# Three chained blocks on one core: the first weights split over two queues, sums of weights by accumulating transfers, and three pieces of early work moved

## The chip, the cores and the metric

The kernel runs on one core of a Trainium2 chip. The metric is the device time of one execution, in microseconds (us). A core has five engines with instruction streams of their own: PE (TensorE, matrix products), DVE (VectorE), ACT (ScalarE), POOL (GpSimd) and SP (SyncE, which here only issues transfers). They meet through semaphores alone. Data live in SBUF; products land in PSUM, 8 banks of 128 x 512 words here.

## The reference

Three blocks follow each other. Attention, with 4 batches, 8 heads, 512 tokens, 32 states and width 64, reads in both directions:

```python
scores = scale * x @ state.T;  a = softmax(scores);   xread = a @ state
scores2 = scale * state @ x.T; a2 = softmax(scores2); sread = a2 @ x
x = concat([xread, sread]) laid out as 2176 rows of 512
```

Then two feed-forward blocks:

```python
x = ((x @ w_a) * (x @ w_b)) @ w_out         # 512 -> 1536 -> 512
h = x @ w_in                                # 512 -> 2048
out = (max(h, 0) + log1p(exp(-abs(h)))) @ w_out2
```

Weights and results have twice the words that fp32 needs: the loaded weights are read as pairs of 32-bit words, a low and a high one, and turned into fp32 on the chip.

## The kernel before, in words

All work is written down as steps of a planner (class `Plan`, lines 156 to 330) in the order of the program. A step has a cost per engine that may do it, the buffers that it reads and writes, and a rank, its place in the program. `go` then goes through modelled time: whenever an engine is free, it gets the ready step of the lowest rank for which buffers can be found. The result is a fixed order of instructions for each engine; at run time the engines follow these orders and wait on semaphores. A step that writes a buffer comes behind every earlier step that wrote the same buffer. Buffers are slots of 128 x 512 words: `SF` holds fp32 (36 slots), `SR` the rounded parts that PE multiplies (58 slots), `PS` is PSUM.

Weights come in 34 units (line 548 on): `ab` (s, 0 and 2), four of the eight quarters of `w_a` and `w_b` that part s of the 1536 columns needs, 6 parts; `wo` (s), the rows of `w_out` of that part; then `in` and `out` for the last block, 8 each. `load` (517) issues the transfers of a unit, on SP except for the very first unit, which both go out on ACT's queue. `fetch` (569) loads whatever stands ahead of a unit in the list and hands the unit to `convert` (529): one ACT activation and, on DVE, two tensor_scalars (line 443), two scalar_tensor_tensors (447) and a tensor_tensor (435, called at 543) that adds the value `v` and the low part `e`. `split` (509) then makes of the sum a rounded high part (a cast on ACT or DVE, 427) and a low rest (a tensor_tensor on DVE or POOL, 435). A product of two split operands is three matmuls (`three`, 484); where an operand is left whole it is one product in full fp32.

At the start x and state arrive (`load_x`, 586). `scores_of` (653) turns x and multiplies it with the state; `state_softmax` (731) makes the softmax over the states, 6 DVE operations of full size among others, and for batches 0 and 1 (`G32`) keeps the result whole for part 0, while `A_later` holds the step that splits it for the parts after. `sread` (682) does the other direction. `state_w` (770) and, from part 1 on, `state_rows` (799) multiply the state with the weights; the results of `state_rows` are laid out by 8 copies of 128 KB on SP for each call. The main loop (979 to 1022) goes over the 6 parts and the 4 batches; `gates_of` (870) computes a part's two products for a batch and multiplies them on DVE (line 887). `y_part` (898) adds the part's share of y. The last block follows (1028 to 1111).

What sets the order around the change: the program's order of the steps `bring_wo(0)`, `bring(s + 1, ...)` and `A_later[b]()`; the queue of SP, which is in order and holds loads and copies alike; and the planner's costs for a transfer (`go`, lines 288 to 290): it lands 1.8 us after its issue plus its bytes at 350 GB/s plus 0.7.

Of the kernel before, what the change touches and what calls it, by code (L numbers as in the profile page):

```python
# [16 lines left out]

P = 128
W = 512
NF_SLOTS = 36  # L20
NR_SLOTS = 58

# [95 lines left out]
def made(x):  # L120
    return x.ap() if isinstance(x, Ref) else x
# [212 lines left out]
def attention_moe_moe2(ctx, tc, x, state, w_a, w_b, w_out, w_in, w_out2, out):  # L334
# [98 lines left out]
    def tt(o, a, b, op):  # L433
        n, ps = cols(o), in_psum(a, b)
        put = lambda eng: lambda: eng.tensor_tensor(  # L435
            out=made(o), in0=made(a), in1=made(b), op=op)
        ways = {"dve": (dve_us(n, True), put(nc.vector), *([] if ps else [True]))}
        if not ps:
            ways["pool"] = (0.23 + 0.00215 * n, put(nc.gpsimd))
        plan.add(ways, [a, b], [o])  # L440
# [19 lines left out]
    def transfer(size, *pairs, act=False):  # L460

        def give():
            for o, i in pairs:
                (nc.scalar if act else nc.sync).dma_start(out=made(o), in_=made(i))  # L464

        ways = {"sp": (0.48 * len(pairs), give, size)}
        if act:
            ways = {"act": (0.45 * len(pairs), give, size, "dma")}
        plan.add(ways, [i for _, i in pairs], [o for o, _ in pairs])

    class Products:


# [40 lines left out]

    raws = []

    def load(n, *srcs, act=False):

        b = Buf(F, 2 * n, RAW_SPARE)
        words = b.all().rearrange("p a b -> p (a b)").bitcast(U32)  # L520
        pairs = []
        for i, src in enumerate(srcs):
            src = src.rearrange("(k p) c -> p k c", p=P).bitcast(U32)
            dst = words.rearrange("p (k i c) -> p k i c", i=len(srcs), k=src.shape[1])
            pairs.append((dst[:, :, i, :], src))
        transfer(2 * n * W * P * 4, *pairs, act=act)
        return b

    def convert(b, spare=0):

        run = b.run // 2
        words = b.all().rearrange("p a b -> p (a b)").bitcast(U32)
        words = words.rearrange("p (c t) -> p c t", t=2)
        low, high = words[:, :, 0], words[:, :, 1]
        v, e = Buf(F, run, spare + run), Buf(F, run, spare)
        v_, e_ = (i.all().rearrange("p a b -> p (a b)") for i in (v, e))
        vu, eu = v_.bitcast(U32), e_.bitcast(U32)
        activation(v_, high.bitcast(F32), AF.Copy, scale=2.0 ** -112)
        ts(vu, vu, 3, ALU.logical_shift_left)
        stt(vu, high, 0x80000000, vu, ALU.bitwise_and, ALU.bitwise_or)  # L540
        ts(eu, vu, 0xFF800000, ALU.bitwise_and)
        stt(e_, low, 2.0 ** -52, e_, ALU.mult, ALU.mult)
        tt(v_, v_, e_, ALU.add)
        return v


# [21 lines left out]

    def fetch(key, spare=0):
        load_to(key)  # L570
        return convert(loaded.pop(key), spare)


    key = order.pop(0)
    loaded[key] = load(*units[key], act=True)
    zs = Buf(F, 1)
    transfer(10 * NS * DM * 4, *(
        (zs[0][NS * b:NS * b + NS].rearrange("p (h d) -> p h d", h=H),
# [74 lines left out]
    def scores_of(b):  # L653

        xT = []
        for g in range(2):
            ps = turned(xs[b], 2 * g)
            xT.append(Buf(F, 2))  # L660
            copy(xT[g].all(), ps.all())
        banks = Buf(K, 2)
        for g in range(2):
            m = Products()
            for i in range(4):
                at = quarter(b, i)
                j, i2 = divmod(i, 2)
                for half in range(2):
                    rows = slice(64 * half, 64 * half + 64)
                    m.one(  # L670
                        banks[half][32 * at:32 * at + 32, g * HW:g * HW + HW],
                        srow(sts[i2 ^ half], 2 * g + j, half, NS * b, NS),
                        xT[g][j][rows, i2 * HW:i2 * HW + HW], True, True, us=0.06,
                        tile_position=(64 * half, 32 * at),
                    )
            m.end()
        raw[b] = Buf(F, 2)
        both = raw[b].all().rearrange("p g (c h n) -> p g c h n", h=2, n=P)
        for half in range(2):
            copy(both[:, :, :, half], banks[half].rearrange("p (g c n) -> p g c n", g=2, n=P))  # L680
# [85 lines left out]
    def bring(s, p):  # L766

        ab[s, p] = ab[s, p + 1] = fetch(("ab", s, p), 4)
# [101 lines left out]
    def gates_of(s, b):  # L870

        m_ = [sw.pop((s, b, g)) for g in range(2)]
        if s:
            m_ = [(i[0], i[1]) for i in m_]
        t = Buf(F, 2)
        for i in range(2):
            ps = Buf(K, 2)
            for k in range(2):
                m = Products()
                c = slice(i * HW + k * P, i * HW + k * P + P)  # L880
                for g in range(2):
                    m.three(ps[k], [q[:, c] for q in m_[g]], A[b][g], g == 0, g == 1)
                m.end()
            if i == 0:
                copy(t.all(), ps.all())
            else:
                tt(t.all(), t.all(), ps.all(), ALU.mult)
        if s == 0 and b in G32:
            A_later[b]()
        return (t,) if s == 0 and b in Y32 else split(t)  # L890

    def add_up(dst, ps, new):
# [86 lines left out]
    for s, b in steps:  # L979
        if s == 0 and b == 0:  # L980
            scores_of(1)
        hl = gates_of(s, b)
        if s == 0:
            if b == 0:
                bring_wo(0)
                state_softmax(1)
                scores_of(2)
                state_w(0, 1, 0)
                state_w(0, 1, 1)
            if b == 1:  # L990
                state_softmax(2)
                scores_of(3)
            if b == 2:
                state_softmax(3)
        if s == SREAD:
            sread(b)
        if s and b == 0:
            if s > SREAD + 1:
                read_x(s)
            bring_wo(s)  # L1000
        if s == SREAD + 1 and b < SREAD + 2:
            read_x(b)
        if s == SREAD + 1 and b == 3:
            for t in range(SREAD + 1):
                read_y(t)
        if s > SREAD and b == 2:
            read_y(s)
        if s + 1 < NHS:
            if b == 0:
                bring(s + 1, 0)  # L1010
            if b == 1:
                bring(s + 1, 2)
                state_rows(s + 1, 0)
            if b == 2:
                state_rows(s + 1, 1)
                state_rows(s + 1, 2)
            if b == 3:
                state_rows(s + 1, 3)
        elif b:
            bring_w2(("in", 0) if b == 1 else ("out", 0) if b == 2 else ("in", 1))  # L1020
        pend.append((s, b, hl))
        if len(pend) > 1:
            finish()
# [122 lines left out]
```

## Time and profile before

| | |
|---|---|
| median of 3 runs | 746.11 us (745.89 to 746.93) |
| profiled execution | 746.87 us, span of its instructions 745.1 us |
| busy: PE, DVE, ACT, POOL | 723.4, 594.3, 409.4, 9.0 us |
| bytes moved by DMA | 66.15 MB, mean 89 GB/s |
| chain that ended last | PE 90%, DVE 4%, SP's queue 2%, DMA 2% |

The span is the time from the first to the last instruction in the trace; the execution's own time has 1.8 us more around it. Busy times are of one execution. An engine that is busy all the time in a stretch sets the length of that stretch; one with idle time waits there for another, and the trace names whom.

### The profile page before, as it was taken

To read this page: it belongs to the slowest core of one execution; us is meant where nothing else is said; L and a number is where in the kernel's file an instruction comes from. 1 tells how busy PE (TensorE), PEld (TensorE's weight loads), DVE (VectorE), ACT (ScalarE), POOL (GpSimd) and SP (SyncE) were. 2 spreads that over 40 slices of the span, in tenths; PEclk is the share of its full clock that TensorE was granted. 3 is DMA by queue.
4 is the path that set the end of the run, shared out by engine and by line. 5 is a ranking of instruction groups with operands and counts; after the bars stand their busy time and mean duration, and the time that the engine had idled before them with its cause. 6 is when DMAs were issued, how large, how long until landed. Compare 5 with 4: busy or idle time off the path is not lost.

```text
span 745.1 us, 9666 instructions
## 1 busy us (share of the span) xinstructions
PE 723.4 (97%) x3776; PEld 589.0 (79%) x3776; DVE 594.3 (80%) x761; ACT 409.4 (55%) x651; POOL 9.0 (1%) x10
## 2 busy tenths in 40 slices
PE   5889999999999999999999999999999999999996
PEld 4457767778787887888888898888988889888895
DVE  4999959898969979987998776567996888875663
ACT  5768854333424324334486676655765657665562
POOL 0000100000000000000010000001000000000000
PEclk9999999999999999999999999999999999999999
DMA  9412654566455465553011003000030111001112
GB/s 306 161 58 61 161 175 141 138 166 177 99 135 162 114 170 169 120 166 104 7 57 56 1 1 114 0 1 0 1 114 1 56 50 64 0 2 57 56 57 70
DMA packets 35152, 66.15 MB, mean 89 GB/s; under 512 B 4772, under 2 KB 8868, under 8 KB 35108
## 3 DMA queue, kind: packets, MB, share of 16 engines
q1 hardware_dynamic: 34564, 64.50, 29.9%
q10 hardware_dynamic: 544, 1.05, 0.4%
q8 instruction: 29, 0.48, 0.3%
q14 instruction: 15, 0.12, 0.0%
HBM read 40.11 MB, written 4.46 MB: 60 GB/s over the span
## 4 chain that ended last, share of the span: by engine, by line
PE 90%; DVE 4%; SPq 2%; DMA 2%; issue 1%; ACT 0%; DVEq 0%; ACTq 0%
PE PS L481 88%; SPq L464 2%; PE PS L496 2%; DVE SF L435 2%; DMA x<-in_x 1%; DVE SF L447 1%; DMA SF<-in_moe_w_b 1%; DVE SR L435 1%; DVE SM L453 0%; DVE SF L443 0%; DVE xf L435 0%; ACT SF L420 0%; ACT SF L427 0%; ACT SR L427 0%; DVE SM L458 0%
## 5 line engine op out<-in xcount | busy, mean ns | idle before, releaser
L481 PE MATMUL PS<-SR 128*128 128x512 f32 (+3 forms) x2134 | 521.5, 378 | 0.0
L481 PEld LDWEIGHTS PS<-SR 128*128 128x128 f32 (+1 forms) x2134 | 376.5, 188 | 73.2 <-issue 5.3
L481 PE MATMUL PS<-xr,SR 128*128 128x512 f32 (+1 forms) x644 | 201.2, 392 | 0.0
L420 ACT ACTIVATE SF<-SF 128x512 f32<-128x512 f32 (+3 forms) x207 | 135.3, 663 | 18.0 <-DMA SF<-in_moe_w_b 12.5
L481 PEld LDWEIGHTS PS<-xr,SR 128*128 128x128 f32 (+1 forms) x644 | 118.4, 188 | 26.7 <-issue 1.3
L427 ACT CAST SR<-SF 128x1024 fp32r<-128x1024 f32 (+3 forms) x103 | 77.6, 756 | 87.5 <-DVE SF L435 82.6
L435 DVE TENSOR_TENSOR SF<-SF,PS 128x1024 f32<-128x1024 f32 (+2 forms) x111 | 104.5, 947 | 25.0 <-PE PS L481 21.8
L427 ACT COPY SF<-PS 128x1024 f32<-128x1024 f32 (+3 forms) x92 | 64.2, 722 | 100.1 <-PE PS L481 90.6
L447 DVE SCALAR_TENSOR_TENSOR SF<-SF 128x1024 uint32<-128x1024 uint32 (+4 forms) x113 | 107.2, 950 | 1.0
L435 DVE TENSOR_TENSOR SR<-SF,SR 128x1024 fp32r<-128x1024 f32 (+3 forms) x95 | 77.5, 822 | 19.9 <-ACT SR L427 19.6
L481 PE MATMUL PS<-SR,xr 128*128 128x512 f32 (+2 forms) x258 | 75.8, 385 | 0.0
L447 DVE SCALAR_TENSOR_TENSOR SF<-PS,SF 128x512 f32<-128x512 f32 (+2 forms) x67 | 40.2, 600 | 41.7 <-ACT SF L420 41.7
L435 DVE TENSOR_TENSOR SF<-SF 128x512 f32<-128x512 f32 (+3 forms) x79 | 63.0, 800 | 1.4
L481 PEld LDWEIGHTS PS<-SR,xr 128*128 128x128 f32 x258 | 48.3, 188 | 9.7 <-issue 0.4
L443 DVE TENSOR_SCALAR SF<-SF 128x1024 uint32<-128x1024 uint32 x57 | 39.2, 688 | 19.7 <-ACT SF L420 19.4
L420 ACT ACTIVATE SF<-PS 128x512 f32<-128x512 f32 (+2 forms) x65 | 34.3, 530 | 36.0 <-PE PS L481 35.1
L427 ACT CAST xr<-SF 128x1024 fp32r<-128x1024 f32 (+1 forms) x24 | 21.3, 887 | 22.1 <-DVE SF L435 22.1
L496 PE MATMUL PS<-ident,SF 128*128 128x128 f32 (+1 forms) x128 | 19.0, 284 | 11.7 <-DMA SF<-in_state 7.8
L481 PE MATMUL PS<-SF 64*32 64x256 f32 (+2 forms) x232 | 27.7, 496 | 1.5 <-ACT SF L427 1.1
L496 PEld LDWEIGHTS PS<-ident,SF 128*128 128x128 f32 (+1 forms) x128 | 15.1, 144 | 17.2 <-issue 9.7
L435 DVE TENSOR_TENSOR SR<-PS,SR 128x1024 fp32r<-128x1024 f32 (+2 forms) x20 | 19.8, 991 | 3.7 <-ACT SR L427 3.7
L481 PEld LDWEIGHTS PS<-SF 64*32 64x32 f32 (+1 forms) x232 | 10.5, 126 | 14.2 <-issue 10.0
(61 smaller groups left out, 350.6 us busy)
## 6 DMA issues: line engine op xcount, KB each, us to landing
SF<-in_moe_w_out SPq DMA_DIRECT2D x14, 1024.0 KB, 5.0
SF<-in_moe_w_in SPq DMA_DIRECT2D x8, 1024.0 KB, 5.5
SR<-xr SPq DMA_DIRECT2D x62, 128.0 KB, 2.3
SR<-SR SPq DMA_DIRECT2D x54, 128.0 KB, 2.3
SF<-in_moe_w_a SPq DMA_DIRECT2D x11, 512.0 KB, 4.4
SF<-in_moe_w_b SPq DMA_DIRECT2D x11, 512.0 KB, 5.1
x<-in_x SPq DMA_DIRECT2D x8, 512.0 KB, 9.9
out<-SF SPq DMA_DIRECT2D x14, 256.0 KB, 2.5
```

The source lines that it names most:

```text
L420: give = lambda: nc.scalar.activation(made(o), made(i), func, **{k: made(v) for k, v in kw.items()})
L427: "act": (act_us(n, ps), lambda: nc.scalar.copy(made(o), made(i))),
L435: put = lambda eng: lambda: eng.tensor_tensor(out=made(o), in0=made(a), in1=made(b), op=op)
L443: give = lambda: nc.vector.tensor_scalar(made(o), made(i), s1, None, op0=op0)
L447: give = lambda: nc.vector.scalar_tensor_tensor(out=made(o), in0=made(a), scalar=s, in1=made(b), op0=op0, op1=op1)
L464: (nc.scalar if act else nc.sync).dma_start(out=made(o), in_=made(i))
L481: self.all.append(lambda: nc.tensor.matmul(made(o), made(w), made(x), start=first, stop=last, **kw))
L496: self.all.append(lambda: nc.tensor.transpose(made(o), made(i), ident))
```

## The change

Five edits. The first unit is loaded with one transfer on each of two queues, `w_a` on ACT and `w_b` on SP, as two steps. `accumulate` is new: a transfer issued by POOL that adds `e` to `v` in SBUF; `convert` uses it in place of the tensor_tensor for all units but the two of part 0. The split of the first two softmaxes (`A_later`) is called ahead of the gates of part 1 instead of behind those of part 0. `bring_wo(0)` and `bring(1, 0)` are called one batch later. Two slots go from `SR` to `SF`.

```diff
-NF_SLOTS = 36
-NR_SLOTS = 58
+NF_SLOTS = 38
+NR_SLOTS = 56
...
+    def accumulate(o, i):
+
+        give = lambda: nc.gpsimd.dma_start(out=made(o), in_=made(i), accum_op=ALU.add)
+        plan.add({"pool": (1.0, give, 3 * P * cols(o) * 4, "dma")}, [o, i], [o])
+
...
-    def load(n, *srcs, act=False):
+    def load(n, *srcs, both=False):
...
-        transfer(2 * n * W * P * 4, *pairs, act=act)
+        size = 2 * n * W * P * 4
+        if both:
+            transfer(size // 2, pairs[0], act=True)
+            transfer(size // 2, pairs[1])
+        else:
+            transfer(size, *pairs)
         return b
 
-    def convert(b, spare=0):
+    def convert(b, spare, key):
...
         stt(e_, low, 2.0 ** -52, e_, ALU.mult, ALU.mult)
-        tt(v_, v_, e_, ALU.add)
+        if key[:2] == ("ab", 0):
+            tt(v_, v_, e_, ALU.add)
+        else:
+            accumulate(v.all(), e.all())
         return v
...
-        return convert(loaded.pop(key), spare)
+        return convert(loaded.pop(key), spare, key)
...
-    loaded[key] = load(*units[key], act=True)
+    loaded[key] = load(*units[key], both=True)
...
-        if s == 0 and b in G32:
-            A_later[b]()
         return (t,) if s == 0 and b in Y32 else split(t)
...
+        if s == 1 and b in G32:
+            A_later[b]()
         hl = gates_of(s, b)
         if s == 0:
             if b == 0:
-                bring_wo(0)
                 state_softmax(1)
...
             if b == 1:
                 state_softmax(2)
                 scores_of(3)
+                bring_wo(0)
...
-            if b == 0:
+            if b == 0 and s:
                 bring(s + 1, 0)
             if b == 1:
+                if s == 0:
+                    bring(s + 1, 0)
                 bring(s + 1, 2)
```

Line numbers grow by up to 15; the matmul of line 481 stands at 486, POOL's copy of 619 at 632, the accumulating transfer at 473. What the planner makes of it, at three places (numbers behind a tile's name are its own; x0 to x3 are the batches of x, xr0 to xr2 the space of x0 to x2 used again for rounded parts):

SP's queue at the start of the program, before; ACT's queue has `w_a` and `w_b` of the first unit there:

```order
L464 DMA SF_64<-in_state 32x8x64 x4
L464 DMA x0_82<-in_x 128x4x256 x2
L464 DMA SF_64<-in_moe_w_a 128x2x512
L464 DMA SF_64<-in_moe_w_b 128x2x512
L464 DMA x1_87<-in_x 128x4x256 x2
L464 DMA SF_64<-in_moe_w_out 128x2x1024
```

and now, with the first unit's `w_a` alone on ACT's queue:

```order
L464 DMA SF_64<-in_state 32x8x64 x4
L464 DMA x0_81<-in_x 128x4x256 x2
L464 DMA SF_64<-in_moe_w_a 128x2x512
L464 DMA SF_64<-in_moe_w_b 128x2x512
L464 DMA x1_86<-in_x 128x4x256
L464 DMA SF_64<-in_moe_w_b 128x2x512
L464 DMA x1_86<-in_x 128x4x256
L464 DMA SF_64<-in_moe_w_out 128x2x1024
```

The single `w_b` between the halves of x1 is the first unit's; the pair ahead of it is the second unit's.

POOL's instructions behind the building of the identity, before:

```order
masks.py:199 AFFINE_SELECT ident_69<-ident_69 128x128
L619 COPY SF_64<-SF_64 128x512
L435 TENSOR_TENSOR SR_65<-SF_64,SR_65 128x1024
L435 TENSOR_TENSOR SF_64<-SF_64,xf_929 128x1024
L435 TENSOR_TENSOR SF_64<-SF_64 128x1024
```

and now (32 transfers in all, 8 of them in the first row with DMA):

```order
masks.py:199 AFFINE_SELECT ident_69<-ident_69 128x128
L632 COPY SF_64<-SF_64 128x512
L435 TENSOR_TENSOR SF_64<-SF_64 128x1024
L435 TENSOR_TENSOR SR_65<-SF_64,SR_65 128x1024 x2
L473 DMA SF_64<-SF_64 128x1024 x8
L473 DMA xf_926<-SF_64 128x1024
L435 TENSOR_TENSOR xr0_716<-SF_64,SR_65 128x1024
```

The first tensor_tensor is the sum of the second unit's weights, and three of them now stand ahead of the transfers.

SP's queue from part 1's second weights (the first pair) to part 2's first (the last pair), before:

```order
L464 DMA SF_64<-in_moe_w_a 128x2x512
L464 DMA SF_64<-in_moe_w_b 128x2x512
L464 DMA SR_65<-SR_65 32x2x512 x8
L464 DMA SF_64<-in_moe_w_out 128x2x1024
L464 DMA SR_65<-xr0_633 32x2x512 x8
L464 DMA xr1_665<-SR_65 32x2x512 x2
L464 DMA SR_65<-SR_65 32x2x512 x4
L464 DMA xr0_633<-SR_65 32x2x512 x2
L464 DMA xr1_665<-xr2_752 32x2x512 x2
L464 DMA SR_65<-xr2_752 32x2x512 x4
L464 DMA xr0_633<-xr2_752 32x2x512 x2
L464 DMA SF_64<-in_moe_w_a 128x2x512
```

and now:

```order
L464 DMA SF_64<-in_moe_w_a 128x2x512
L464 DMA SF_64<-in_moe_w_b 128x2x512
L464 DMA SF_64<-in_moe_w_out 128x2x1024
L464 DMA SR_65<-SR_65 32x2x512 x2
L464 DMA xr0_716<-SR_65 32x2x512 x4
L464 DMA SR_65<-SR_65 32x2x512 x2
L464 DMA SR_65<-xr1_720 32x2x512 x2
L464 DMA xr0_716<-xr1_720 32x2x512 x4
L464 DMA SR_65<-xr1_720 32x2x512 x2
L464 DMA SF_64<-in_moe_w_a 128x2x512
L464 DMA SF_64<-in_moe_w_b 128x2x512
L464 DMA SR_65<-xr2_772 32x2x512 x8
```

Between part 1's second weights and part 2's first stood 32 copies; now there are 16.

## Rows read from the trace of the kernel before

**Rows 1.** Page, busy us, share of the span and instructions of each engine.

```profile
PE 723.4 (97%) x3776; PEld 589.0 (79%) x3776; DVE 594.3 (80%) x761; ACT 409.4 (55%) x651; POOL 9.0 (1%) x10
```

**Rows 2.** Windows: length; busy us of PE, PEld, DVE, ACT, POOL; PE clock, DMA share, GB/s.

```profile
7.83:15.00 7.17, 6.94 (x56) 5.51 (x64) 5.61 (x6) 4.42 (x7) 0.61 (x1) 1.00 1.08 363
...
20.00:30.00 10.00, 7.59 (x120) 4.36 (x109) 9.93 (x12) 7.59 (x10) 0.00 (x0) 1.00 0.74 249
30.00:40.00 10.00, 8.89 (x33) 4.50 (x32) 9.93 (x12) 6.53 (x7) 0.00 (x0) 1.00 0.01 2
40.00:50.00 10.00, 8.89 (x32) 5.18 (x30) 9.96 (x14) 6.52 (x9) 0.00 (x0) 0.83 0.00 0
...
41.66:45.07 3.41, 3.41 (x11) 2.38 (x12) 3.41 (x5) 2.91 (x4) 0.00 (x0) 0.50 0.00 0
...
100.00:120.00 20.00, 18.16 (x74) 13.42 (x73) 14.22 (x16) 10.38 (x12) 0.00 (x0) 1.00 0.56 191
...
200.00:300.00 100.00, 100.00 (x457) 79.64 (x456) 84.06 (x81) 34.70 (x37) 0.00 (x0) 1.00 0.56 149
...
738.00:745.10 7.10, 0.00 (x1) 0.00 (x0) 0.73 (x2) 0.00 (x0) 0.00 (x0) 0.74 0.55 179
```

**Rows 3.** Timeline of PE: start, us, instructions, idle before and its releaser.

```profile
7.83 1.09 PE L496 MATMUL PS<-ident,SF 128*128 128x128 f32 x4 [7.83 <-DMA SF<-in_state]
...
39.37 1.06 PE L496 MATMUL PS<-ident,SF 128*128 128x128 f32 x8 [0.87 <-DVE SF L435]
41.55 1.91 PE L496 MATMUL PS<-ident,x 128*128 128x128 f32 x8 [1.11 <-DVE SF L435]
```

**Rows 4.** Chain of waits (start, us, what), and three rows of the timeline.

```profile
2.66 6.44 DMA x<-in_x
...
23.23 1.13 DVE SF L447
24.36 0.60 DVE SF L443
...
27.22 0.10 DVE SM L443
...
27.35 0.36 DVE SM L458
...
40.36 1.14 DVE SF L435
...
7.12 1.13 ACT L420 ACTIVATE SF<-SF 128x1024 f32<-128x1024 f32 x1 [5.10 <-DMA SF<-in_moe_w_b]
8.28 0.73 DVE L443 TENSOR_SCALAR SF<-SF 128x1024 uint32<-128x1024 uint32 x1 [8.28 <-ACT SF L420]
10.92 0.68 DVE L435 TENSOR_TENSOR SR<-SF,SR 128x512 fp32r<-128x512 f32 x1
```

**Rows 5.** Timeline of SP's queue, one step of the chain, and PE, 81 to 111.

```profile
81.10 5.07 SPq L464 DMA_DIRECT2D SR<-xr  x8
...
98.25 5.09 DMA SF<-in_moe_w_b
...
110.41 0.44 PE L496 MATMUL PS<-ident,SF 128*128 128x128 f32 x2 [1.84 <-DVE SF L435]
```

**Rows 6.** Timeline of POOL and DVE around POOL's first tensor_tensor.

```profile
75.00 2.41 POOL L435 TENSOR_TENSOR SR<-SF,SR 128x1024 fp32r<-128x1024 f32 x1 [66.53 <-ACT SR L427]
...
75.15 3.33 DVE L435 TENSOR_TENSOR SF<-SF,SM 128x1024 f32<-128x1024 f32 x1
79.81 1.22 DVE L435 TENSOR_TENSOR xr<-PS,xr 128x1024 fp32r<-128x1024 f32 x1
```

**Rows 7.** DMA issues: tiles, queue, count, KB each, median us to landing.

```profile
SF<-in_moe_w_out SPq DMA_DIRECT2D x14, 1024.0 KB, 5.0
...
SR<-SR SPq DMA_DIRECT2D x54, 128.0 KB, 2.3
```

**Rows 8.** Groups by line: DVE's tensor_scalars, busy us, mean ns.

```profile
L443 DVE TENSOR_SCALAR SF<-SF 128x1024 uint32<-128x1024 uint32 x57 | 39.2, 688 | 19.7 <-ACT SF L420 19.4
```

## The prediction

> **What bounds the kernel now.** I read the busy times first. TensorE (PE) is busy 723.4 of 745.1 us [rows 1]. Then I cut the span into windows: in 200 to 300 us PE is busy in all of the window, DVE in 84.1 of 100 us [rows 2], and the windows from 120 to 700 us look the same for PE. No work taken from another engine can shorten those stretches. So a gain has to come from PE's idle time, and that is a short list: 7.83 us before the first matmul, which waits for the state [rows 3]; 2.41, 1.11 and 1.11 us in 20 to 30, 30 to 40 and 40 to 50; 1.84 us in 100 to 120; a tail of 7.1 us behind 738 [rows 2]. Add one stretch at half clock, 41.66 to 45.07, where the granted clock is 0.50 (1.2 of 2.4 GHz) right after PE had idled 0.87 and 1.11 us [rows 2, 3]: 3.41 us with the work of 1.70. I take the tail as unchanged (17 output transfers end both programs). The most that could be won is then about 7.8 + 6.5 + 1.7 = 16 us.
>
> The chain of waits says who holds PE back. From about 23 to 41.50 us it is DVE nearly without a break, and its last step there is the gates multiply at 40.36 [rows 4]. The third place is the load of part 2's weights: SP issues it at 98.25, it lands 5.09 us later, ACT and DVE convert it, and DVE is then late with a product that PE waits for until 110.41 [rows 5].
>
> **The change, part by part.**
>
> *The first weights.* The words say "ahead of state". The order says otherwise for one half: w_b of the first unit stands on SP behind the state, both halves of x0, both second weights and half of x1; only w_a is still early, on ACT. The planner saw both transfers write the same buffer and let the second wait for the first. So 512 KB leave the front of the stream. The stream runs at 363 GB/s [rows 2], so 524 kB are 1.44 us: the first matmul should come at about 6.4 instead of 7.83 us, x0 at 7.7 instead of 9.10 [rows 4]. That is 1.4 us, if DVE, which is next, keeps up.
>
> *DVE up to the gates multiply.* In both orders that multiply is DVE's 33rd row. Before: 22 full-size operations at 1.13, 6 tensor_scalars at 0.60, one half-size at 0.68 and two pairs of a tiny tensor_scalar and a reciprocal, 0.50 with the steps between [rows 4]: 24.9 + 3.6 + 0.7 + 1.0 = 30.2 us of work, from 8.28 to 41.50, so 3.0 us of waiting in it. After: 20 full-size, 5 tensor_scalars, the half-size one, two pairs and three tiny ones (0.4 together): 22.6 + 3.0 + 0.7 + 1.0 + 0.4 = 27.7. The first unit's five operations are still there; w_out's conversion has gone behind, and one of the two adds has gone to POOL. But DVE can start later: it now begins with the second weights, which in the old stream land at about 9.10 + 3 x 1.44 = 13.4, in the new one at 12.0. With ACT's 1.13 us [rows 4] DVE starts at 13.1 rather than 8.28. Less the half-size operation done meanwhile: 13.1 + 27.0 = 40.1, that is 1.4 us earlier than 41.5.
>
> *POOL's tensor_tensors.* Before, POOL's first one is at 75.00 us, and DVE's multiply that began beside it took 3.33 instead of 1.22 us, to 1.07 us behind POOL's end [rows 6]: it stood still for 2.1 us. Now three of them come ahead of POOL's first DMA, and the first is one of DVE's adds in just this list. One block puts the multiply at 42.2, 0.7 us later than before. The two values, 40.1 and 42.2, lie on both sides of 41.5; I take their middle, -0.3 us for the whole early stage, start included, since the 1.4 us at the start is worth only what DVE lets through. Bounds: -3.4 (the 1.4, and both idles of 0.87 and 1.11 gone) and +3.7 (DVE waits 3.0 us as before on top of one block: 45.2).
>
> *The half clock.* It followed the idle around 40 us. With more scores placed ahead of the gates PE should not idle there, but it may now idle around 18 to 22, while x1 and x2 land. Bounds 0 and -1.7, and nothing shows where it will fall; the middle is -0.8.
>
> *The next weights (unit `ab` 1) and w_out later, part 2's weights earlier.* Behind the weights of part 1, SP used to issue 32 copies of 128 KB ahead of part 2's first weights; now 16. Eight take 5.07 us [rows 5], so the load is issued about 10 us sooner and has that much in hand against the 1.84 us stall. I take the stall as gone, -1.8. Bounds: 0 (the buffer is not free sooner) and the whole 1.8.
>
> *The accumulating transfers.* 32 of the 34 units lose their DVE add: 32 x 1.13 = 36 us of DVE time, nearly all where PE is full, so worth 0. What they cost is latency: the sum used to be there after 1.2 us, now after a DMA. The trace of before has no such DMA. Nearest rows: a copy of 128 KB inside the chip lands in 2.3 us, a load of 1024 KB in 5.0 [rows 7], so 2.7 us for each further 896 KB. A sum of 512 KB counted once is 2.3 + 1.2 = 3.5 us; counted three times, as read, read and write, 2.3 + 4.2 = 6.5. POOL's issue adds some 0.6, as a copy's on SP [rows 5]. So 4.1 to 7.1; I take the upper half, 6, since the destination has to be read too. The planner's entry (1.8, 1.5 MB at 350 GB/s, 0.7) lets a consumer follow 7.0 us behind the issue. Within that, ACT's cast finds its input, PE sees nothing: 0. Cover beyond it: a group of six matmuls on PE is 1.3 us (457 in 100 us [rows 2]), so from about 8.3 us on it costs. No gain is possible, PE being full.
>
> *The softmax parts.* The splits of the first two softmaxes move from behind their gates of part 0 to ahead of those of part 1: the same operations, out of the early stage. That is in the DVE list above; where they go PE is full. Two slots more of one kind and two less of the other only act through the order. 0.
>
> A rule of the Trainium skill speaks against the accumulates. What the row shows is POOL holding DVE up [rows 6]. Its page SBUF — State Buffer (section "SBUF: two separate sides", the trap "DVE blocks DMA") states the reverse too: a transfer issued by GpSimd cannot write its descriptors while DVE runs an operation in a two-port mode. No run here shows it yet. DVE's candidates are the 57 tensor_scalars of 0.69 us [rows 8], so by the rule an accumulate comes at most about 0.7 us later, 6.7 instead of 6, and the sum stays; at the upper end, 7.8, it would use up more than half of the cover.
>
> **Sum.** -0.3 - 0.8 - 1.8 = -2.9 us. The profiled execution took 746.87, so 744.0; the median of the runs shown, 746.11, lies 0.76 lower, so I forecast 743.2.
>
> **The rivals.**
> 1. *The accumulate is late: slower.* Place: ACT's cast of the summed weights, behind which ACT's PSUM copies queue, in order. For: loads of weights share the DMA engines, 0.56 of whose time is taken in 200 to 300 us [rows 2]; 512 KB of other data in between are 1.4 us, which with the upper end of 7.1 makes 8.5. Against: that takes the worst of everything, and a cast that the order puts later has more in hand. It decides from 8.3 us on. If it takes 10 us and a third of the 32 casts follow as closely as the planner allows (an estimate, no row shows it): 11 x 1.7 = 18.7 us on top of the forecast, 762. At 9.1 us it is 11 x 0.8 = 8.8, 752.
> 2. *The early stage eats it: no change.* POOL holds DVE twice (4.2 us) or the late first w_b leaves DVE waiting, and the half clock falls elsewhere: +2 instead of -1.1, with the 1.8 of the stall 746.3. For: POOL has three such operations there. Against: only an operation of DVE that starts inside one is held.
> 3. *The stall at 108 us stays or moves:* -1.1 alone, 745.0, no change. For: SP's queue is in order and a load waits for its buffer there. Against: ten us in hand.
>
> **How the numbers follow.** Forecast 0.60, rival 1 0.20, rival 2 0.13, rival 3 0.07. By the rule on descriptors rival 1 would get 0.25. The two programs can be told apart from about 0.2%, 1.5 us: faster is below 744.6, slower above 747.6. Faster is the forecast, 0.60; slower is rival 1 and a quarter of rival 2, 0.23; the same is the rest, 0.17. The range leaves out a little over one in ten at the top (rival 1 above 9.1 us) and less than that below: all lower bounds together, -3.4 - 1.7 - 1.8, would be 739.2. So 740.0 to 752.0; the forecast alone would be 740.0 to 744.6.
>
> **What would show it.** First matmul at 6.2 to 6.8 us. DVE starting on the second weights at about 13. POOL's tensor_tensors between 20 and 50 us, and a DVE operation of over 3 us beside one. No PE idle over 1 us in 95 to 125, part 2's weights issued near 88. DVE busy near 557 us instead of 594 [rows 1]. In the list of waits, ACT behind the accumulated buffers (a transfer between two SF buffers) in total below 10 us. I am wrong if those waits come to tens of us and PE shows gaps of 1 us and more after 160 (rival 1), or if PE's idle before 50 us is as long as now or longer (rival 2).

## The result, and the profile after

The changed kernel takes **755.63 us** (median of 4 runs, 754.22 to 757.92) beside 746.07 for the kernel before on the same chip: ratio 1.0125, 95% interval 1.0100 to 1.0151. It is slower, and outside the range given (740.0 to 752.0). Its profiled execution, the longest of the four, took 757.92 us, with a span of 755.9. Executions in the chip's slower state are left out of every time given here.

The page of the changed kernel, busy us by engine, to be held against [rows 1]:

```profile
PE 726.5 (96%) x3776; PEld 589.2 (78%) x3776; DVE 558.2 (74%) x727; ACT 406.6 (54%) x650; POOL 44.3 (6%) x45
```

DVE lost its 36 us, as forecast, and PE was not helped by it. Windows of the changed kernel, with the columns of [rows 2]:

```profile
20.00:30.00 10.00, 6.92 (x88) 5.08 (x88) 10.00 (x11) 5.18 (x8) 2.75 (x1) 0.83 0.98 337
30.00:40.00 10.00, 8.79 (x74) 4.06 (x59) 8.96 (x8) 8.47 (x12) 2.35 (x1) 1.00 0.02 6
...
100.00:120.00 20.00, 16.14 (x58) 11.43 (x57) 10.38 (x12) 6.72 (x9) 1.73 (x2) 0.91 1.04 243
112.26:115.67 3.41, 3.41 (x9) 2.67 (x10) 3.35 (x4) 0.00 (x0) 0.00 (x0) 0.51 1.09 244
200.00:300.00 100.00, 99.03 (x449) 79.01 (x447) 72.60 (x71) 33.81 (x36) 4.32 (x5) 1.00 0.72 174
300.00:400.00 100.00, 97.49 (x437) 79.28 (x437) 82.61 (x90) 47.55 (x62) 3.87 (x5) 1.00 0.47 120
```

In 100 to 120 us PE is busy 16.14 us where it was 18.16, the DMA share is 1.04 where it was 0.56, and a second stretch at half clock (granted clock 0.51) follows the idle. From 200 to 400, where PE was full, it now idles 3.5 us. PE's timeline, the rows with an idle time ahead that matter:

```profile
6.31 1.08 PE L501 MATMUL PS<-ident,SF 128*128 128x128 f32 x4 [6.31 <-DMA SF<-in_state]
...
14.13 1.09 PE L501 MATMUL PS<-ident,x 128*128 128x128 f32 x8 [1.19 <-DMA x<-in_x]
...
19.18 0.67 PE L486 MATMUL PS<-SF 64*32 64x256 f32 x16 [1.10 <-ACT SF L427]
22.57 1.10 PE L501 MATMUL PS<-ident,x 128*128 128x128 f32 x8 [2.72 <-DMA x<-in_x]
...
105.60 0.44 PE L501 MATMUL PS<-ident,SF 128*128 128x128 f32 x2 [1.16 <-DVE SF L435]
...
112.16 2.35 PE L486 MATMUL PS<-SR 128*128 128x512 f32 x5 [2.70 <-DMA SR<-SR]
...
368.91 0.50 PE L486 MATMUL PS<-SR 128*128 128x512 f32 x1 [1.75 <-ACT SR L427]
```

Worked out from the whole of such a timeline, the end of PE's last matmul splits into its start, its idle times, the half clock (a stretch of 3.41 us holds the work of 1.7) and the rest, which is matmuls at full clock:

```
                 start  idle to 60  60 to 130  after 130  half clock  matmuls  end
before            7.83        4.86       1.89       0.00         1.7    721.7  738.0
changed           6.31        8.49       3.86       3.48         3.4    723.1  748.7
e9_part2_small    6.42        7.73       0.85       0.73         1.7    722.6  740.1
e10_both_small    6.37        7.75       0.00       0.00         1.7    723.0  738.8
e13_behind        6.70        7.77       0.19       1.46         1.7    723.8  741.6
e18_sp66          8.17        4.68       0.06       0.00         1.7    721.3  735.9
```

The changed kernel ends 10.7 us later: 1.5 won at the start, 3.6 lost up to 60 us, 2.0 lost around 105, 3.5 lost behind 200, 1.7 by the second half clock, and 1.4 in the matmuls themselves, which I can't explain. (Each kernel has a further low-clock stretch behind its last matmul, which costs nothing.)

The chain of waits of the changed kernel at two places (start, us, what):

```profile
97.11 7.47 DMA SR<-xr
...
104.62 7.41 DMA SR<-SR
...
112.16 1.92 PE PS L486 x4
```

```profile
334.41 8.93 DMA SF<-SF
...
343.37 1.06 ACT SR L427
...
356.59 7.67 DMA SF<-SF
...
364.28 1.06 ACT SR L427
...
367.81 1.05 ACT SR L427
```

The first is not the weights but the 128 KB copies that lay out the products of the state: 7.4 us each time, where such a copy landed in 2.3 [rows 7]. SP's queue shows what stands ahead of them:

```profile
89.77 2.13 SPq L464 DMA_DIRECT2D SR<-xr  x2
92.02 1.75 SPq L464 DMA_DIRECT2D SF<-in_moe_w_a  x1
93.87 0.86 SPq L464 DMA_DIRECT2D SF<-in_moe_w_b  x1
94.82 7.78 SPq L464 DMA_DIRECT2D SR<-xr  x8
102.65 0.58 SPq L464 DMA_DIRECT2D SF<-in_moe_w_a  x1
103.30 0.48 SPq L464 DMA_DIRECT2D SF<-in_moe_w_b  x1
103.98 7.33 SPq L464 DMA_DIRECT2D SR<-SR  x8
```

Before, the first of part 2's weights left here:

```profile
97.63 0.52 SPq L464 DMA_DIRECT2D SF<-in_moe_w_a  x1
```

Part 2's weights, issued 5.6 us earlier, now stand ahead of part 1's last copies, the first pair ahead of 16, the second of 8. The second place is the accumulating transfers. Their medians on the page (count, KB each, us to landing):

```profile
SF<-SF POOLq DMA_DIRECT2D x27, 512.0 KB, 6.1
...
SR<-xr SPq DMA_DIRECT2D x38, 128.0 KB, 5.1
```

The median of 6.1 us is the 6 of the prediction; the two in the chain took 8.93 and 7.67, and all 32 lie between 4.5 and 10.0.

### The profile page after: what moved, and what is told of

Its sections match the earlier page's. It is cut to its first block, busy times and chain, and to the rows that moved or that the text cites. A ratio compares the mean times of both kernels' runs of the same rounds, so it can differ in the third digit from the quotient of the medians.

```text
span 755.9 us, 9762 instructions
## 1 busy us (share of the span) xinstructions
PE 726.5 (96%) x3776; PEld 589.2 (78%) x3776; DVE 558.2 (74%) x727; ACT 406.6 (54%) x650; POOL 44.3 (6%) x45
## 3 DMA queue, kind: packets, MB, share of 16 engines
q0 software_dynamic: 4608, 16.78, 11.5%
## 4 chain that ended last, share of the span: by engine, by line
PE 79%; DMA 8%; DVE 7%; SPq 3%; issue 1%; ACT 1%; DVEq 0%; POOLq 0%; ACTq 0%
PE PS L486 78%; SPq L464 3%; DVE SF L435 2%; DMA SF<-SF 2%; DMA x<-in_x 2%; DVE SR L435 1%; PE PS L501 1%; DMA SF<-in_moe_w_in 1%; DVE SF L447 1%; DMA SR<-xr 1%; DMA SR<-SR 1%; DMA SF<-in_moe_w_a 1%; ACT SR L427 1%; DVE SM L453 1%; DVE SM L443 0%
## 5 line engine op out<-in xcount | busy, mean ns | idle before, releaser
L486 PE MATMUL PS<-SR 128*128 128x512 f32 (+3 forms) x2310 | 546.2, 381 | 6.7 <-DMA SR<-SR 2.7
L486 PEld LDWEIGHTS PS<-SR 128*128 128x128 f32 (+1 forms) x2310 | 410.8, 188 | 91.5 <-issue 11.1
L427 ACT CAST SR<-SF 128x512 fp32r<-128x512 f32 (+3 forms) x110 | 86.6, 790 | 113.3 <-DVE SF L435 92.3
L486 PE MATMUL PS<-SR,xr 128*128 128x512 f32 (+2 forms) x510 | 145.4, 382 | 0.0
L435 DVE TENSOR_TENSOR SF<-SF,PS 128x512 f32<-128x512 f32 (+2 forms) x123 | 113.7, 935 | 31.8 <-PE PS L486 28.5
L486 PEld LDWEIGHTS PS<-SR,xr 128*128 128x128 f32 x510 | 94.7, 188 | 18.4 <-DVE SF L435 0.4
L447 DVE SCALAR_TENSOR_TENSOR SF<-SF 128x512 f32<-128x512 f32 (+4 forms) x117 | 99.8, 857 | 0.6
L486 PE MATMUL PS<-xr,SR 128*128 128x512 f32 (+1 forms) x232 | 73.6, 392 | 0.0
L473 POOL DMA_DIRECT2D SF<-SF x27 | 23.7, 876 | 482.7 <-DVE SF L447 235.7
L486 PEld LDWEIGHTS PS<-xr,SR 128*128 128x128 f32 (+1 forms) x232 | 42.1, 188 | 9.5 <-issue 1.1
L501 PEld LDWEIGHTS PS<-ident,SF 128*128 128x128 f32 (+1 forms) x128 | 15.8, 147 | 14.1 <-issue 7.1
```

Of the source, the lines that this page charges most:

```text
L427: "act": (act_us(n, ps), lambda: nc.scalar.copy(made(o), made(i))),
L435: put = lambda eng: lambda: eng.tensor_tensor(out=made(o), in0=made(a), in1=made(b), op=op)
L447: give = lambda: nc.vector.scalar_tensor_tensor(out=made(o), in0=made(a), scalar=s, in1=made(b), op0=op0, op1=op1)
L473: give = lambda: nc.gpsimd.dma_start(out=made(o), in_=made(i), accum_op=ALU.add)
L486: self.all.append(lambda: nc.tensor.matmul(made(o), made(w), made(x), start=first, stop=last, **kw))
L501: self.all.append(lambda: nc.tensor.transpose(made(o), made(i), ident))
```

## The experiments

I began with two theories. **A**: the accumulating transfers cost it, by coming late and by the DMA time that they take. **B**: the moved loads and the late first `w_b` cost it, in the early stage. The first four kernels each hold a part of the change. Each time is a median of 4 to 10 runs; the ratio is to the kernel before on the same chip, with its 95% interval.

**e1, the accumulates alone in the kernel before.**

```diff
-        tt(v_, v_, e_, ALU.add)
+        if key[:2] == ("ab", 0):
+            tt(v_, v_, e_, ALU.add)
+        else:
+            accumulate(v.all(), e.all())
```

> The kernel before with the accumulating transfers alone. Theory A (their lateness and their share of the DMA engines cost most of the 9.6 us): 752 to 757 us, with ACT waiting for the accumulated buffers and copies of 128 KB landing later than 2.3 us. Theory B (the moved loads and the late first w_b cost it, the transfers little): 745 to 747 us.

759.61 us, ratio 1.0179 (1.0162 to 1.0196): worse than the whole change and above theory A's range. Its largest idle is 4.41 us at 177, and the chain of waits leads again to a copy:

```profile
173.16 6.00 DMA SR<-xr
179.25 0.06 ACT xr L427
...
181.23 0.79 PE PS L486
```

No load stands just ahead of this copy. What was issued beside it is an accumulating transfer, at 172.47, and behind it a load, at 173.79; the four copies issued from 169.96 to 171.87 landed in 2.3 to 2.4 us.

**e2, the change without the accumulates** (the hunk of e1 undone).

> The changed kernel without the accumulating transfers, the sums on DVE or POOL as before; all else as in the change. Theory A: 743 to 747 us, near the kernel before. Theory B: 752 us or more, the stalls at 104 to 112 us and in the first 35 us still there.

754.49 us, 1.0111 (1.0093 to 1.0129).

**e3, only the two queues for the first unit.**

```diff
-    loaded[key] = load(*units[key], act=True)
+    loaded[key] = load(*units[key], both=True)
```

> The kernel before with the first unit's load split over two queues alone. Theory A: within 1.5 us of 746. Theory B: 748 to 750 us, first matmul near 6.3 us as in the change, but PE idle of some 8 us instead of 4.9 between it and 60 us, since the first unit's w_b lands behind x1's first half.

754.57 us, 1.0110 (1.0095 to 1.0125).

**e4, only the moved steps** (`A_later`, `bring_wo(0)` and `bring(1, 0)`, as in the change).

> The kernel before with the three moved steps alone (softmax splits, w_out's first unit, part 1's first weights). Theory A: 743 to 746 us, the DVE-bound early stage a little shorter. Theory B: 749 us or more, with part 2's loads between the copies of 128 KB and a stall of several us near 105 to 112 us.

755.86 us, 1.0139 (1.0114 to 1.0163). Each part alone costs 8 to 13 us, and they don't add up to the 9.6 of the whole. Both theories fall as they were put. So I formed **theory C**: the planner writes a new order of the whole program for any edit, the order of before is a good one, and a new order costs some 10 us whatever the edit is. Two edits that take away or add no work test it, and two runs on the changed kernel:

**e5, only the slots.**

```diff
-NF_SLOTS = 36
-NR_SLOTS = 58
+NF_SLOTS = 38
+NR_SLOTS = 56
```

> The kernel before with 38 and 56 slots in place of 36 and 58, and none of the other four edits: no operation is added or taken away, but the planner, which picks slots and steps as they come free, writes another order for all five engines. Theory C (what costs is that the program is planned anew; the order of before is a good one that the new ones don't reach, whatever the edit is): 751 to 760 us, with PE idle in new places after 60 us. Theory A (the accumulating transfers) and theory B (the moved loads and steps): both say 746 us within 1.5, since neither is here.

756.13 us, 1.0122 (1.0100 to 1.0144). Neither theory A nor theory B has a place in this kernel. The same operations in another order lose 10 us. The largest idle is, in PE's timeline,

```profile
107.54 0.77 PE L481 MATMUL PS<-SR,xr 128*128 128x512 f32 x1 [4.92 <-DMA xr<-SR]
```

again a copy, at the place of the changed kernel's.

**e6, one number of the planner.**

```diff
-        return 0.165 + (0.00086 if psum else 0.0009) * n
+        return 0.170 + (0.00086 if psum else 0.0009) * n
```

> The kernel before with one number of the planner changed: the fixed cost of an ACT operation, 0.165 to 0.170 us. The same operations, the same order on SP's queue, some 220 matmuls and 320 DVE operations at other places. Theory C: slower, but by less than the wholly new orders, 747.5 to 755 us. Theories A and B: 746 us within 1.5.

746.41 us, 1.0000 (0.9990 to 1.0011). Against theory C: this order, with SP's queue unchanged, costs nothing.

**e7, the changed kernel's order, the accumulates cut to an eighth.**

```diff
-        give = lambda: nc.gpsimd.dma_start(out=made(o), in_=made(i), accum_op=ALU.add)
+        give = lambda: nc.gpsimd.dma_start(out=made(o)[:, 0, 0:W // 4], in_=made(i)[:, 0, 0:W // 4], accum_op=ALU.add)
```

> The changed kernel, its order held as it is, but each accumulating transfer moves only the first 128 of 1024 words of a row (so seven eighths of the low parts are left out of the sums). Theory A (the accumulates are late, or take DMA time from others): the idle of 0.97 us at 249 and of 2.51 us at 367 to 370 goes, the copies at 95 to 112 are issued faster, together 4 to 8 us: 748 to 751.5 us. Theory C with the accumulates as the cause of only what the gaps behind 200 show: 752 us, that is 3.5 less than the changed kernel. If the accumulates cost nothing in this order: 755.6 within 1.5.

749.56 us, 1.0062 (1.0039 to 1.0084), within theory A's numbers. The median says little here, since five of the nine runs took 748.8 to 749.6 us and four 752.3 to 754.4. By the two ratios, 1.0125 and 1.0062, the accumulates' bytes are worth some 4.7 us (an estimate) with the order held. The profiled run is one of the four (754.31), 3.6 below the changed kernel's. In it the idle times behind 200 us are gone; the one at 108 stays (3.38 us, behind a copy). Against the expectation, the copies among part 2's loads land no sooner: issued between 94.5 and 112 us, their medians are 7.6 and 8.6 us, against 7.5 and 7.3 in the changed kernel. The small accumulates land in 3.0 us by the page:

```profile
SF<-SF POOLq DMA_DIRECT2D x27, 64.0 KB, 3.0
```

**e8, the changed kernel with the number of e6.**

> The changed kernel with the planner's fixed cost of an ACT operation at 0.170 instead of 0.165 us: all five edits, in another order. Theory C: another draw, 749 to 760 us, with PE's gaps in other places than 104, 109 and 367. If the changed kernel's 755.6 is the price of its edits (theory A or B): 755.6 within 1.5, with the gaps at the same places.

765.56 us, 1.0243 (1.0207 to 1.0278), with new idle times of 4.20 us at 100, 2.30 at 205 and 3.29 at 332. The same edits, planned with one number changed by 3%, cost 10 us more, outside both expectations.

The place that e1, e5, e7 and the changed kernel share is a copy that comes late. **Theory D**: loads of part 2 on SP's queue ahead of part 1's copies fill the DMA engines, the copies come late, PE waits and falls to half clock.

**e9, the changed kernel's order, part 2's four loads cut to 64 of 1024 words of a row.**

```diff
+                if few:
+                    o, i = o[:, 0:1, 0:W // 8], i[:, 0:1, 0:W // 8]
...
-            loaded[k] = load(*units[k])
+            loaded[k] = load(*units[k], few=k[:2] == ("ab", 2))
```

> The changed kernel, its order held, but each of the four loads of part 2's w_a and w_b moves 64 of 1024 words of a row (the rest of those weights is left out). Theory D (the two rows of eight 128 KB copies at 95 to 112 us come late because these loads, now issued ahead of and among them on SP's queue, take the DMA engines; PE then waits 1.16 and 2.70 us and runs 3.41 us at half clock): the copies land in 2 to 3 us again, PE's idle from 95 to 130 falls from 3.86 to below 0.6 and the half clock at 112 goes: 755.6 - 3.5 - 1.7 = 750.4, so 749 to 752 us. If the copies are late because of the accumulates: 755.6 within 1.5.

750.04 us, 1.0043 (1.0028 to 1.0057): 5.6 us of the loss hang on these four loads. SP's queue issues the copies at 0.63 to 0.70 us each again (0.92 to 0.97 in the changed kernel, stalls included):

```profile
94.11 5.56 SPq L467 DMA_DIRECT2D SR<-xr  x8
...
100.89 5.08 SPq L467 DMA_DIRECT2D SR<-SR  x8
```

and those issued between 94.5 and 112 us land as fast as before (count, KB each, median us to landing):

```profile
SR<-xr SPq DMA_DIRECT2D x8, 128.0 KB, 2.3
SR<-SR SPq DMA_DIRECT2D x8, 128.0 KB, 2.3
```

In the changed kernel the same rows have 7.5 and 7.3. PE is busy in all of 100 to 120 us. The idle at 367 is gone as well, with the accumulates at full size; so e7's 4.7 and e9's 5.6 overlap. An accumulating transfer delays copies too: the two copies issued just behind one, from 89 to 91 us, land in 5.7 us in the changed kernel, in 6.0 here, and in 2.9 in e7.

**e10, both cuts.**

> The changed kernel, its order held, with both cuts: the accumulates at 128 of 1024 words and part 2's four loads at 64 of 1024. Theory D with A (in this order the loss is the late copies and the late accumulates, and the early stage is about even): 749.6 - 3.4 - 1.7 = 744.5, so 743.5 to 746 us, no more than the kernel before. If the early stage (14.8 us of idle up to 60 us against 12.7, and its half clock) is a loss as well: 747 us or more.

747.48 us, 1.0010 (0.9999 to 1.0021): no idle is left behind 60 us, and the kernel is within 0.2% of before. That is 8.2 of the 9.6 us. Of what is left the early stage has the most, start and idle together 14.1 against 12.7 us.

**e11, nothing left out, but ACT issues the four loads.**

```diff
-                (nc.scalar if act else nc.sync).dma_start(out=made(o), in_=made(i))
+                (nc.scalar if act or other else nc.sync).dma_start(out=made(o), in_=made(i))
...
+            loaded[k] = load(*units[k], other=k[:2] == ("ab", 2))
```

> The changed kernel, nothing left out, its order held but for the four loads of part 2's w_a and w_b, which ACT issues instead of SP, at the places where the planner put them. Theory D in the form that a copy stands behind a load in the same queue: the copies at 95 to 112 land in 3 us, 750 to 752 us. If it is the DMA engines' time and not the queue: copies still take 6 us or more, 754 to 757 us.

755.12 us, 1.0106 (1.0087 to 1.0124). No load of part 2 stands between the copies in SP's queue any more, and a copy is as slow as in the changed kernel. The chain of waits:

```profile
88.52 7.46 DMA xr<-xr
...
113.74 7.50 DMA xf<-in_moe_w_out
...
127.41 2.80 PE PS L486 x7
```

ACT's first two loads go out at 87.92 and 88.39, and the copy of 88.52 lands beside them in 7.46 us. PE waits only 0.9 us at the copies now, since the loads have gone 4 us earlier; SP then comes late to w_out, and PE idles 0.97 and 1.70 us for that at 124 to 127. So a second queue moves the wait and takes away little of it: it is the DMA engines that are shared. The Trainium skill states this on its page DMA: Bandwidth & Descriptors, section "Issuing engines are not separate DMA queues": transfers started by any engine run on the same 16 DMA engines and interleave. The 7.46 us agree.

**e12, the kernel before with a truer cost of an issue on SP in the planner** (eight copies take 5.07 us [rows 5]).

```diff
-        ways = {"sp": (0.48 * len(pairs), give, size)}
+        ways = {"sp": (0.63 * len(pairs), give, size)}
```

> The kernel before with the planner's cost of one issue on SP set to what the trace shows for a copy, 0.63 instead of 0.48 us (eight take 5.07). All operations as before, another order. Theory C (each new order costs some 10 us): 751 to 760 us. If orders lose by what the planner has wrong about SP's queue: 743 to 747 us, with PE's idle at 108 us gone.

**744.29 us, 0.9967 (0.9955 to 0.9979)**: faster than both kernels. The loads stand behind the 32 copies as before and leave no earlier (98.08 us, where it was 97.63), and the 1.84 us of idle at 108 [rows 5] are gone; the window shows PE full:

```profile
100.00:120.00 20.00, 20.00 (x83) 14.94 (x81) 15.95 (x18) 10.92 (x12) 0.00 (x0) 1.00 0.60 208
```

**e13, the changed kernel, nothing left out, the loads of part 2 and later planned behind part 1's copies.**

```diff
+            for p in behind:
+                step.after.add(p)
+                p.before.append(step)
...
+            loaded[k] = load(*units[k], behind=laid if k[1] > 1 or k[0] in ("in", "out") else ())
```

(`laid` holds the steps that issue part 1's copies.)

> The changed kernel with nothing left out; the planner is told that loads of part 2 and later come behind the 32 copies of part 1, so SP issues all 32 and then the weights (planned anew, some 3,500 of the matmuls at other places). Theory D (the loads ahead of the copies cost 5.6 us, by e9): the idle in 95 to 130 falls to 2 us or less and the time to 749 to 752 us. Theory C (any new order costs what it costs): 749 to 766 us, as the orders so far, with the idle wherever it falls.

750.05 us, 1.0051 (1.0036 to 1.0066), as much as e9 gave by leaving the loads out. Both expectations hold this time, and the order is a new one, so it is the idle time that speaks. SP's queue:

```profile
90.29 9.32 SPq L464 DMA_DIRECT2D SR<-xr  x10
99.70 5.08 SPq L464 DMA_DIRECT2D SR<-SR  x8
104.82 0.59 SPq L464 DMA_DIRECT2D SF<-in_moe_w_a  x1
```

The loads leave at 104.82, 12.8 us later than in the changed kernel and 7 later than in the one before, and PE idles only 0.19 us between 95 and 130, as theory D said. In this order part 2's weights are not needed early.

**e14, the changed kernel with e12's number.**

> The changed kernel with the planner's cost of one issue on SP at 0.63 instead of 0.48 us, all five edits, nothing left out. If orders lose by what the planner has wrong about SP's queue (as e12 suggests): 748 to 752 us. If they lose by the DMA engines' time, which the number does not tell the planner (loads still stand among the copies in this order): 753 to 760 us.

750.88 us, 1.0060 (1.0043 to 1.0076). Its loads still stand among the copies, for which theory D's expectation was 753 or more. But it idles nowhere between 95 and 130, and 5.9 us in 60 to 95 and 130 to 200 together. So loads among the copies need not hold PE up there.

**e15, the changed kernel without accumulates, with e12's number and e13's edit.**

> The changed kernel without the accumulates (DVE adds as before), with 0.63 us for an issue on SP and the loads of part 2 and later behind the copies of part 1. Theories A and D together (late accumulates and late copies are the loss, the moved steps cost nothing): 744 to 748 us. Theory B (the moved steps and the late first w_b cost by themselves): 750 us or more, with the idle before 60 us.

749.83 us, 1.0048 (1.0033 to 1.0063), between the two expectations: idle of 3.4 us between 60 and 95, none from 95 to 400. Neither theory holds all of it. What is left of the change here (the moved steps, the split first load, the slots) costs something in this order; no run tells which of them.

**e16, the slots alone with e12's number.**

> The kernel before with 38 and 56 slots and 0.63 us for an issue on SP, none of the other edits. Loads of part 2 still stand ahead of the last 8 of part 1's 32 copies in this order. Theory D: those 8 copies land late, so some of the 10 us stays: 749 to 754 us. If the planner's SP cost was the whole of it: 744 to 748 us.

751.63 us (749.09 to 753.55), 1.0066 (1.0042 to 1.0090), where e5 had 756.13. Some of the loss stays, as theory D said, but its idle is no longer mainly at the copies (0.77 us at 102, 1.51 at 59), so this is no proof of it.

**e17 and e18, the kernel before with 0.60 and 0.66 in the place of e12's 0.63.**

> The kernel before with 0.60 us for an issue on SP in the planner. Wholly another order on PE (3,500 matmuls at other places), but the four loads of part 2 stand behind all 32 copies of part 1 on SP, as before. Theory D: no late copies, 743 to 748 us. Theory C (a new order costs some 10 us whatever stands in it): 751 us or more.

> The kernel before with 0.66 us for an issue on SP in the planner; again another order, again part 2's loads behind the 32 copies. Theory D: 743 to 748 us, and if a truer cost is what e12 gained by, no more than 746. Theory C: 751 us or more.

745.69 us, 0.9991 (0.9980 to 1.0003), and 744.27 us, 0.9972 (0.9961 to 0.9983). In both, PE has another order than before (some 3,500 matmuls at other places in e17), and nothing is lost. Theory C falls: a new order need not cost anything. In both the idle at 108 us is gone; e17, which idles 0.9 us longer than e18 up to 60 us and 0.5 behind 300, can't be told from the kernel before.

How the idle at 108 us went is seen in DVE's timelines. First the kernel before, then e17:

```profile
104.59 0.69 DVE L443 TENSOR_SCALAR SF<-SF 128x1024 uint32<-128x1024 uint32 x1 [6.14 <-ACT SF L420]
105.20 1.21 DVE L435 TENSOR_TENSOR SF<-SF,PS 128x1024 f32<-128x1024 f32 x1
```

```profile
102.78 1.22 DVE L435 TENSOR_TENSOR SF<-SF,PS 128x1024 f32<-128x1024 f32 x1 [4.06 <-PE PS L481]
104.97 0.69 DVE L443 TENSOR_SCALAR SF<-SF 128x1024 uint32<-128x1024 uint32 x1 [0.97 <-ACT SF L420]
```

In the kernel before, DVE waited for the weights, and a step on the way to PE's next product stood behind their conversion; in e17 that step comes first. The loads leave at the same time in both (97.63 and 97.64 us).

## Why the prediction was wrong

*"I take the stall as gone, -1.8."* **This step failed.** It counted what the loads were waiting for and not what would wait for them. The loads did go earlier (92.02 instead of 97.63, where some ten us had been forecast). But 16 copies of part 1 were now beside them on the DMA engines, PE needed those first, and idle of 1.84 us became 3.86, with a stretch at half clock (1.7 us) on top. With the order held, taking the loads' bytes away gave back 5.6 us and brought the copies back to 2.3 (e9); another queue gave nothing beyond 0.5 (e11). Planning them behind the copies gave 5.6 too, in a new order (e13). Nor was an earlier load needed for the stall: in e12, e17 and e18 the loads leave at 97.6 to 98.1 us and it is gone. Rival 3, the stall that "stays or moves", had the place and not the price: it was held to a gain of 1.8 that stays out.

*The accumulating transfers, "0".* The size came out right (6 us forecast, 6.1 measured), but by luck: with nothing beside it an accumulate lands in 4.5 us (at 412, 427, 517 and 617 us, for instance), beside a load of 1024 KB in some 7.7 (at 536), and the median lies between. The step "within that, ACT's cast finds its input, PE sees nothing" failed. The median hides 8.93 and 7.67 us, and the second already reached PE, below my 8.3; both stand in one chain, where the first had used up the cover. Rival 1 had the mechanism. Its price, a third of 32 casts at 0.8 to 1.7 us, was not what happened: three idle times, 3.5 us together, which e7 takes away. In this order all of it is worth some 4.7 us (e7), part of it shared with the loads (e10: 8.2 for both). The late sum alone isn't enough for it: e9 and e11, with accumulates of full size, idle 0.73 and 0.69 us behind 130.

*The early stage, "-0.3, start included".* Measured 2.1 later, within the bounds of -3.4 and +3.7 but at the wrong end. The first matmul came at 6.31, as forecast (6.2 to 6.8), and POOL did hold DVE up, and twice. POOL's and DVE's timelines of the changed kernel:

```profile
24.65 2.75 POOL L435 TENSOR_TENSOR SF<-SF 128x1024 f32<-128x1024 f32 x1 [17.70 <-DVE SM L443]
35.74 2.35 POOL L435 TENSOR_TENSOR SR<-SF,SR 128x1024 fp32r<-128x1024 f32 x1 [8.34 <-ACT SR L427]
...
25.36 3.12 DVE L447 SCALAR_TENSOR_TENSOR SF<-SF 128x1024 f32<-128x1024 uint32 x1
...
36.33 1.80 DVE L443 TENSOR_SCALAR SM<-SM 128x2 f32<-128x2 f32 x1
...
45.08 1.21 DVE L435 TENSOR_TENSOR SF<-SF,PS 128x1024 f32<-128x1024 f32 x1
```

DVE's row of 3.12 us is 1.9 more than its neighbours' 1.22, and its row of 1.80 some 1.7 more than others of that size. The gates multiply ended at 46.3 instead of 41.5, beyond the prediction's bound of 45.2 and 6.2 behind its 40.1: DVE began on the second weights at 14.68 instead of 13.1, POOL held it for 3.6 us in all, and it waited 1.04 us for a cast of ACT. So "POOL holds DVE twice" of rival 2 was right; that DVE waits for the first w_b is not seen. But PE lost most elsewhere: it waited 1.19 and 2.72 us for x at 14 and 22 us, 4.2 us for x in all where it had been 0.2. The prediction named that idle, under the half clock, and gave it no term; its sum followed DVE alone.

*The half clock, "-0.8".* Measured +1.7: the early one moved to 23.6, and a second came at 112, behind the copies. The prediction looked for it only in the early stage.

*DVE's 36 us worth nothing, the softmax parts 0.* The first was right (558.2 forecast 557, and PE, where it is full, took no notice). For the second no run isolates it; e4 shows that the moved steps together, in the order that they led to, cost 9.4 us.

The forecast's own parts that can be read then make +2.1, +2.0, +3.5 and +1.7 in place of -0.3, -1.8, 0 and -0.8. Of the rule on descriptors that spoke against the accumulates no run here shows anything: nothing separates its 0.7 us from the spread between 4.5 and 10.0.

What stays open is why e2, e3, e4 and e15 lose. In e2 to e4 loads of part 2 stand among the copies too, but their largest idle times lie elsewhere (2.96 us at 281 in e4, 2.72 at 36 in e3). The timelines say where PE idles and not why: up to 60 us e2, e3 and e4 idle 7.8, 9.8 and 8.0 us, where the kernel before idles 4.9 (some 8 was theory B's figure for e3), and behind 130 us 2.1, 1.9 and 4.4, where it idles none. Of the kernels with nothing left out, all in which the steps were moved or the loads stood among the copies took 749.8 us or more, and all others (before, e6, e12, e17, e18) 744.3 to 746.4; that is a pattern, and no cause shown for each of them.

## What to carry to other kernels

When a transfer moves forward, list the small transfers that it will now share the DMA engines with, and ask which engine waits for those: a load that nobody needs yet is best issued behind them. When a planner sets the order, cost the order that it writes and not the edit: holding the order and shrinking one kind of transfer told more here than undoing parts of the change, because each undoing wrote another order. Setting a planner's cost that the trace contradicts (0.48 us for an issue that takes 0.63) gave 0.3% at 0.63 and 0.66 and nothing clear at 0.60; e12 and e18 are the versions to keep, and that the truer number is the cause is not shown. Before hastening a load that an engine waits for, ask what that engine has in its order behind the wait: moving that ahead did here what an earlier load did not.

## What the hardware showed that I had not expected

Accumulating transfers are dear in DMA time. The changed kernel's page, by queue (packets, MB, share of 16 engines over the span):

```profile
q1 hardware_dynamic: 34836, 65.03, 30.7%
q0 software_dynamic: 4608, 16.78, 11.5%
```

32 of them took 11.5% of 755.9 us, 2.7 us of all 16 engines each, so 193 GB/s of the bytes added, against 280 for the loads and copies. With nothing beside them they land in 4.5 us, and at an eighth of the bytes the median is still 3.0. And a copy of 128 KB, which lands in 2.3 us at the median in the kernel before, took 7.4 us beside the loads of part 2 in the changed kernel, 7.5 with those loads on ACT's queue (e11), and 6.0 just behind one accumulating transfer (e9).
